# Thresholded attention and a gated MLP on one core: the threshold taken as the sign of differences scaled to 2^-126, one Exp per step over words read as int32, q and k transposed by half tiles, new lists of order

## The chip, the cores and the metric

The kernel runs on one core of one Trainium2 chip. The metric is the device time of one execution in microseconds; the time before is the median of three runs. The profile is one execution, with every instruction's start and duration on each engine: PE (TensorE, matmuls and transposes), PEld (its weight loads), DVE (VectorE), ACT (ScalarE), POOL (GpSimd) and SP, whose queue issues nearly all DMAs. Each engine works through its own row of instructions strictly in order, so an instruction that waits holds up everything behind it on its engine.

## The reference

Eight batches of eight heads, 576 positions, 64 dimensions a head. Scores more than tau = 0.02 below their row's maximum are dropped, the rest go through a softmax; its output goes into an MLP with spatial gating.

```python
scores = scale * np.matmul(q, k.transpose(0, 1, 3, 2))          # scale = 1/8
thresh = np.max(scores, axis=-1, keepdims=True) - tau
scores = np.where(scores >= thresh, scores, -1000000000.0)
scores = scores - np.max(scores, axis=-1, keepdims=True)
attn = np.exp(scores)
attn = attn / (np.sum(attn, axis=-1, keepdims=True) + 1e-09)
x = np.matmul(attn, v)                                          # then (8, 576, 512)
h = np.maximum(x @ w_in, 0.0)                                   # 512 -> 1024, split into u and v
v_n = (v - mu) / np.sqrt(var + 1e-06)
v_s = np.einsum('ts,bsd->btd', w_spatial, v_n) + b_spatial[None, :, None]
out = (u * v_s) @ w_out
```

## The kernel before

**Tiling.** The 64 heads are 32 pairs, four to a batch. A pair's 576 rows give four and a half blocks of 128; the half blocks of two neighbouring pairs share a step, so a batch has 18 steps and the whole kernel 144 (named g; the batch is the iteration). A step handles 128 rows of scores of both heads of a pair, 2 x 576 columns.

**A step.** The letters are those of the lists. S and Y (`part`, L830) make the scores on PE as float32 products of 64x64 tiles in one of two PSUM tiles `s`, three banks each. M (`top`, L859) is a DVE operation for each head that copies 576 scores from PSUM into the ring tile `e` and takes their maximum into `peak`, in SBUF; its second instruction reads the accumulator out. B (`shift`) makes the negative of the maximum plus tau (`negm`), on POOL (L873) or on DVE (L869). Then a step goes one of two ways, given by the table `WAYS`. In way "a" (102 of 144 steps) E and F are an ACT Prelu for each head (L890), which multiplies what is below the threshold by 1e30, and Z (L925) is one Exp over both heads into `p` in float16. In way "n" (42 steps) E and F are already the Exps (L887), and two DVE operations make the threshold: C (`keep`, L909) a mask, A (`pick`, L918) the bitwise AND into `p`. T sends `p` through a DMA transpose into `pT`. P (L505 to L524) multiplies `pT` with v and a column of ones; i (a reciprocal, L545) and p (a product, L548) divide by the sum on DVE.

**Beside the steps.** q and k of a pair are cast into the order of the blocks on POOL (sq, L306), transposed on PE (QA for q, QB for k, four 128x128 float32 transposes each, L448, into one of the two PSUM tiles `f`), and copied out into `qkT` by qa and qb, q times 1/8 (L428 on ACT, L422 on DVE), k as it is (L430, L424). QR, qr and kd do the same for the half blocks (L467, L460). The MLP of the batch before runs between: v with its mean and variance (L656 to L708), u, the gating product s and the output o. All of these share the two `f` tiles, each of one bank.

**Order.** Nothing schedules at run time. `ORDER` has a list of tokens for each batch and `LAST` four for the end; `run_token` issues the instructions of a token, each to its engine's row, so the lists set the order on every engine. A letter d ahead of an eviction puts it on DVE instead of ACT. The wait of an instruction on another engine is a semaphore that the framework places where a tile is written and read.

Of the kernel before, what the change touches and what calls it, by code (L numbers as in the profile page):

```python
# [34 lines left out]
(  # L35
# [18 lines left out]
(  # L54
# [117 lines left out]
(  # L172
# [1090 lines left out]
```

## Time and profile before

| | value |
|---|---|
| time, median of three runs | 429.21 us (428.72 to 431.87) |
| the profiled execution's own time | 429.39 us |
| its span in the trace | 427.6 us |
| POOL, DVE, ACT instructions | 469, 1035, 567 |
| DMA moved, mean rate | 88.18 MB, 206 GB/s |
| transposes of p by DMA | 141, 4.4 us from issue to landing |

The span runs from the first to the last instruction in the trace; 1.8 us of the execution lie outside it. A busy time is the union of an engine's instructions, so that the sums of groups, which overlap by some tens of nanoseconds at their ends, come to more. PE's instructions are pipelined and their ends modelled: a busy PE is not PE at its peak. Views used below are the page's sums by engine and its chain of waits, the groups of instructions by line, the answers for a single line with smallest, median and largest duration, the busy times by stretch of the span, and the timeline.

### The profile page before, as it was taken

What the parts mean: (1) busy time and instruction counts of PE and PEld (TensorE: products, weight loads), DVE (VectorE), ACT (ScalarE), POOL (GpSimd) and SP (SyncE); (2) the same over time, 40 slices, a digit from 0 to 9 for tenths busy, and PEclk for the clock granted to TensorE, in tenths of its full rate; (3) what the DMA queues carried; (4) which work ended last, traced back from release to release, by engine and by line L of the source; (5) the groups of instructions that cost most, each with busy time, mean ns of one, the idle gap of its engine ahead of it and who ended that gap; (6) DMA issues with size and microseconds to landing.
All of it is one profiled execution on the core that took longest, in us unless ns stands there. A gap on an engine that the chain in (4) does not pass through costs nothing.

```text
span 427.6 us, 13266 instructions
## 1 busy us (share of the span) xinstructions
PE 405.0 (95%) x4978; PEld 253.3 (59%) x5029; DVE 384.0 (90%) x1035; ACT 386.1 (90%) x567; POOL 191.4 (45%) x469
## 2 busy tenths in 40 slices
PE   8778978999999999999999999999999999999995
PEld 4456655566555675575665657656665666565642
DVE  6999989999899899989999999989999989999562
ACT  4999979999999999999999999999999999999362
POOL 2566437763246633554235631374233753255020
PEclk9999999999999999999999999999999999999999
DMA  7999999999999999998999989999989999989913
GB/s 196 288 280 182 263 273 227 168 182 195 239 265 171 214 213 188 204 210 227 214 165 280 211 165 252 217 221 210 236 138 229 228 214 206 160 150 214 180 57 117
DMA packets 224703, 88.18 MB, mean 206 GB/s; under 512 B 195648, under 2 KB 220352, under 8 KB 224640
## 3 DMA queue, kind: packets, MB, share of 16 engines
q1 hardware_dynamic: 224192, 86.75, 102.3%
q8 instruction: 39, 0.64, 0.6%
q10 hardware_dynamic: 368, 0.33, 0.2%
q0 software_dynamic: 80, 0.26, 0.2%
q14 instruction: 24, 0.20, 0.2%
HBM read 32.79 MB, written 9.44 MB: 99 GB/s over the span
## 4 chain that ended last, share of the span: by engine, by line
PE 62%; DVE 11%; ACT 9%; DMA 7%; issue 5%; POOL 3%; SPq 1%; POOLq 0%; DVEq 0%; ACTq 0%
PE s L830 25%; DVE e L859 7%; PE f L752 6%; DMA pT<-p 6%; PE f L448 5%; PE f L510 5%; PE f L723 4%; PE f L656 4%; ACT e L890 3%; PE f L781 3%; ACT e L887 2%; PE f L505 2%; ACT p L925 1%; DMA xT<-xn 1%; PE f L641 1%
## 5 line engine op out<-in xcount | busy, mean ns | idle before, releaser
L859 DVE CUSTOM_DVE_ANT_0 e<-s,zero 128x576 f32<-128x576 f32 x288 | 204.3, 752 | 5.8 <-PE s L830 1.4
L830 PE MATMUL s<-qkT 64*64 64x160 f32 (+1 forms) x2304 | 172.9, 413 | 4.5 <-DVE peak L859 3.7
L890 ACT ACTIVATE e<-e,negm 128x576 f32<-128x576 f32 x204 | 148.3, 766 | 4.8 <-PE s L830 2.3
L830 PEld LDWEIGHTS s<-qkT 64*64 64x64 f32 x2304 | 105.3, 132 | 53.2 <-issue 19.1
L925 ACT ACTIVATE p<-e 128x1152 f16<-128x1152 f32 x102 | 117.1, 1157 | 0.8
L873 POOL TENSOR_SCALAR negm<-peak 128x2 f32<-128x2 f32 x93 | 21.5, 231 | 133.3 <-DVE peak L859 89.7
L887 ACT ACTIVATE e<-e,negm 128x576 f16<-128x576 f32 x84 | 62.4, 767 | 2.0 <-POOL negm L873 1.3
L510 PE MATMUL f<-v,pT 128*128 128x65 bf16 x984 | 44.6, 194 | 0.0
L510 PEld LDWEIGHTS <-pT 128*128 128x128 f16 x1024 | 41.9, 98 | 2.4 <-issue 0.6
L918 DVE TENSOR_TENSOR p<-e 128x576 int32<-128x576 int32 x42 | 34.4, 822 | 0.5
L752 PE MATMUL f<-wsT,vn 128*128 128x512 bf16 x121 | 31.9, 380 | 0.9 <-DVE qkT L424 0.2
L505 PE MATMUL f<-v,pT 128*128 128x130 bf16 x123 | 27.2, 221 | 4.0 <-DMA pT<-p 3.9
L333 POOL CAST v<-vl 128x512 bf16<-128x512 f32 x32 | 21.3, 666 | 18.6 <-PE s L830 17.5
L708 POOL TENSOR_SCALAR vn<-vrel,rs,nm 128x512 bf16<-128x512 f32 (+1 forms) x35 | 27.9, 798 | 3.6
L723 PE MATMUL f<-xT,w_in 128*128 128x512 bf16 x102 | 28.5, 380 | 1.0 <-ACT qkT L430 0.3
L656 PE MATMUL f<-w_in,xT 128*128 128x512 bf16 x98 | 27.0, 380 | 1.4 <-DMA xT<-xn 0.3
L548 DVE TENSOR_TENSOR xn<-f,r 128x384 bf16<-128x384 f32 x46 | 25.2, 554 | 0.7
L781 PE MATMUL f<-w_o,gT 128*128 128x512 bf16 x94 | 25.1, 379 | 0.4
L859 DVE DVE_READ_ACCUMULATOR2_ANT peak<- 128x1 f32 x288 | 23.9, 83 | 0.0
L306 POOL COPY qn<-ql 128x512 f32<-128x512 f32 x31 | 19.7, 636 | 5.9 <-DMA ql<-in_q_dram 2.7
L752 PEld LDWEIGHTS <-vn 128*128 128x128 bf16 x140 | 12.8, 98 | 15.5 <-issue 3.1
L448 PE MATMUL f<-identf,kn 128*128 128x128 f32 x124 | 19.8, 282 | 2.2 <-DVE qkT L424 1.5
(175 smaller groups left out, 560.2 us busy)
## 6 DMA issues: line engine op xcount, KB each, us to landing
vl<-in_v_dram SPq DMA_DIRECT2D x16, 512.0 KB, 5.2
ql<-in_q_dram SPq DMA_DIRECT2D x15, 512.0 KB, 5.5
kl<-in_k_dram SPq DMA_DIRECT2D x15, 512.0 KB, 5.7
out_dram<-oo SPq DMA_DIRECT2D x12, 512.0 KB, 4.2
pT<-p SPq DMA_TRANSPOSE x141, 4.4
uT<-in_moe_w_in_dram SPq DMA_DIRECT2D x3, 512.0 KB, 6.4
uT<-in_moe_w_spatial_dram SPq DMA_DIRECT2D x2, 576.0 KB, 6.8
vx<-in_v_dram SPq DMA_DIRECT2D x16, 64.0 KB, 3.8
```

The source lines that it names most:

```text
L448: nc.tensor.transpose(out=t[:, c * P:(c + 1) * P], in_=nat[i][which][:, c, :], identity=identf)
L505: nc.tensor.matmul(out=t[:, at:at + 130], lhsT=pt[:, 4, rows], rhs=vt[:, 4:6, :].rearrange("p b d -> p (b d)"), start=True, stop=False)
L510: nc.tensor.matmul(out=t[:, at + 65 * h:at + 65 * h + 65], lhsT=pt[:, 5 * h + j, rows], rhs=vt[:, 6 * h + j, :], start=False, stop=(h == 1 ...
L656: nc.tensor.matmul(out=t, lhsT=x_of(b, f, slice(c * P, (c + 1) * P)), rhs=w_in[:, f, 512:1024], start=(f == 0), stop=(f == 3))
L723: nc.tensor.matmul(out=t, lhsT=w_in[:, m, f * P:(f + 1) * P], rhs=x_of(b, m, slice(0, 512)), start=(m == 0), stop=(m == 3))
L752: nc.tensor.matmul(out=t, lhsT=vn[:, c, f * P:(f + 1) * P], rhs=wsT[:, c, 0:512], start=(c == 0), stop=(c == 4))
L781: nc.tensor.matmul(out=t[:n], lhsT=gs[b][:, f, c * P:c * P + n], rhs=w_o[:, f, :], start=(f == 0), stop=(f == 3))
L830: made.append(nc.tensor.matmul(out=s_ring[g % 2][halves[k], at[h] + lo:at[h] + hi], lhsT=qks[n][halves[h], 0, m:m + 64], rhs=qks[n][halves ...
L859: nc.vector.tensor_tensor_reduce(out=e_ring[g % 3][:, h, :], in0=view(s_ring[g % 2], at[h], [[1, S]]), in1=zero.broadcast_to([P, S]), scal ...
L887: nc.scalar.activation(out=half_e(g)[0][:, h, :], in_=s, func=ACT.Exp, bias=bias_, scale=scale if steps[g][1] == 4 else 1.0)
L890: nc.scalar.activation(out=e, in_=s, func=ACT.Prelu, bias=bias_, scale=scale if steps[g][1] == 4 else 1.0, alpha=1e30)
L925: nc.scalar.activation(out=numerators(g), in_=e_ring[g % 3].rearrange("p h s -> p (h s)"), func=ACT.Exp)
```

## The change

The threshold moves off ACT. M now multiplies by 1/8 while it copies, and its accumulator goes to the first two columns of the step's own PSUM tile `s`. B is one DVE operation for each step: maximum minus tau, from PSUM into `thr`. E and F, one for each head, compute (score - thr) * 2^-126 in place in `e`, on POOL, or on DVE where the token has a d (180 and 108 of 288). A score above the threshold then is a tiny positive float whose bits, read as an integer, are the difference times 2^23; one below has its sign bit set and reads as a large negative integer. Z, for all 144 steps, is one ACT Exp over 1152 such words read as int32, times 2^-23, minus tau. `WAYS`, C and A are gone. The ring of `e` grows from three tiles to four, that of `p` shrinks from ten to nine.

q and k of a pair are transposed together (QX): each 128x128 block as two transposes of 64 rows, the upper rows into one `f` tile and the lower rows into the other, 16 for a pair where 8 were; qx and qy then copy one `f` tile each, half of q and half of k. q is no longer scaled there. At the start, two tiles go once through the same chain of operations, on POOL and on DVE, and the constant -0.5 (`mhalf`) comes out of that. All lists are new; evictions are nearly all on ACT now.

```diff
+    NE, NP = 4, 9
-    def qk_main(i, which):
+    def qk_main(i):
         def mm():
-            t = hold["t"] = bank()
-            for c in range(4):
-                nc.tensor.transpose(out=t[:, c * P:(c + 1) * P], in_=nat[i][which][:, c, :],
-                                    identity=identf)
+            hold.extend(bank() for _ in range(2))
+            for c in range(8):
+                w, n = divmod(c, 4)
+                for r in range(2):
+                    nc.tensor.transpose(
+                        out=hold[r][:, 64 * c:64 * c + 64], in_=nat[i][w][halves[r], n, :],
+                        identity=identf[halves[r], halves[r]])
+        def ev(r):
+            dst = qk_of(i)[:, :, 64:S].rearrange("p w (c s) -> p w c s", c=4)
+            evict(dst[:, :, :, 64 * r:64 * r + 64],
+                  hold[r].rearrange("p (w c s) -> p w c s", w=2, c=4))
...
+    def top(g):
+        peak[g] = s_ring[g % 2][:, 0:2]
+        for h in range(2):
             nc.vector.tensor_tensor_reduce(
-                in1=zero.broadcast_to([P, S]), scale=1.0, scalar=float("-inf"),
+                in1=zero.broadcast_to([P, S]), scale=scale, scalar=float("-inf"),
                 op0=ALU.add, op1=ALU.max, accum_out=peak[g][:, h:h + 1])
+    def bound(g):
+        thr[g] = small.tile([P, 2], F32, name="thr")
+        nc.vector.tensor_scalar(out=thr[g], in0=peak[g], scalar1=-float(tau), scalar2=None,
+                                op0=ALU.add)
     def spread(g, h):
+        e = e_ring[g % NE][:, h, :]
+        (nc.vector if on_vector[0] else nc.gpsimd).tensor_scalar(
+            out=e, in0=e, scalar1=thr[g][:, h:h + 1], scalar2=2.0 ** (SHIFT - 149),
+            op0=ALU.subtract, op1=ALU.mult)
     def exps(g):
-        nc.scalar.activation(out=numerators(g), in_=e_ring[g % 3].rearrange("p h s -> p (h s)"),
-                             func=ACT.Exp)
+        nc.scalar.activation(out=numerators(g),
+                             in_=e_ring[g % NE].rearrange("p h s -> p (h s)").bitcast(I32),
+                             func=ACT.Exp, bias=wrap, scale=2.0 ** -SHIFT)
...
+        for n, eng in enumerate((nc.gpsimd, nc.vector)):
+            t = e_ring[n][:, 0, :]
+            nc.vector.memset(t, 2.0 ** -100)
+            eng.tensor_scalar(out=t, in0=t, scalar1=zero, scalar2=2.0 ** -30,
+                              op0=ALU.subtract, op1=ALU.mult)
+            nc.scalar.activation(out=t, in_=t.bitcast(I32), func=ACT.Identity, scale=-2.0 ** -20)
+        nc.vector.tensor_tensor(out=mhalf, in0=e_ring[0][:, 0, 575:576],
+                                in1=e_ring[1][:, 0, 575:576], op=ALU.max)
```

SHIFT is 23 here. How the rows stand, at three places; names end in the number of the buffer, `s_96` and `s_97` are the two score tiles, `f_91` and `f_92` the two shared ones.

PE where a pair of the middle batches is transposed, before: eight full transposes behind scores of two steps.

```order
L830 MATMUL s_96<-qkT 64x416 x4
L830 MATMUL s_97<-qkT 64x160 x2
L830 MATMUL s_97<-qkT 64x416 x4
L448 MATMUL f_91<-identf,kn 128x128 x4
L448 MATMUL f_92<-identf,qn 128x128 x4
L830 MATMUL s_96<-qkT 64x160 x2
```

The same kind of place after; sixteen rows of the last kind follow one another, eight of q and eight of k, in turn into the two tiles.

```order
L810 MATMUL s_96<-qkT 64x160 x2
L810 MATMUL s_96<-qkT 64x416 x4
L810 MATMUL s_96<-qkT 64x160 x2
L440 MATMUL f_92<-identf,qn 128x64
L440 MATMUL f_91<-identf,qn 128x64
```

Each transpose has 64 rows in and 64 columns out of the identity, and both `f` tiles are taken at once.

DVE at its start, before, up to the copies of the first k and q:

```order
L1185 MEMSET zero 128x1
L1188 MEMSET ntau 128x1
L1189 MEMSET mhalf 128x1
L1191 CAST identb<-identf 128x128
L1192 CAST identh<-identf 128x128
L321 COPY kn<-kl_139 128x512
L321 COPY qn<-ql_138 128x512
```

And after; the maximum (L1128) waits for two ACT instructions, of which one waits for POOL.

```order
L1120 MEMSET zero 128x1
L1121 MEMSET wrap 128x1
L1124 MEMSET e_106 128x576
L1124 MEMSET e_107 128x576
L1125 TENSOR_SCALAR e_107<-e_107,zero 128x576
L1128 TENSOR_TENSOR mhalf<-e_106,e_107 128x1
L1131 CAST identb<-identf 128x128
L1132 CAST identh<-identf 128x128
L308 COPY kn<-kl_138 128x512
L308 COPY qn<-ql_137 128x512
```

Four operations of `e` and `mhalf` now stand ahead of the first copies of k and q.

DVE within a middle batch, before (M is named ISA here, two rows for each head):

```order
L859 ISA e_109,peak<-s_97,zero 128x576
L859 ISA peak 128x1
L909 TENSOR_SCALAR e_107<-e_107 128x2x576
L424 COPY oo<-f_91 128x512
L675 BN_STATS st<-vrel 128x6
L918 TENSOR_TENSOR p_111<-e_107 128x576
L859 ISA e_107,peak<-s_96,zero 128x576
```

And after:

```order
L846 TENSOR_SCALAR thr<-s_97 128x2
L665 BN_STATS st<-vrel 128x6
L538 TENSOR_TENSOR xn<-f_91,r 128x384
L665 BN_STATS st<-vrel 128x6
L669 BN_AGGR mv<-st 128x2
L852 TENSOR_SCALAR e_106<-e_106,thr 128x576
L838 ISA e_107,s_97<-s_97,zero 128x576
```

The mask, the AND and the copy of the output are gone from this row; the threshold and a spread of `e` stand in it. POOL beside it, before, where it normalises v (rs, nm, vn):

```order
L703 TENSOR_SCALAR nm<-mv,rs 128x1
L708 TENSOR_SCALAR vn_136<-vrel,rs,nm 128x512
L460 COPY qkT<-qkT 64x64
L873 TENSOR_SCALAR negm<-peak 128x2 x2
L696 TENSOR_SCALAR rs<-mv 64x1
L701 TENSOR_TENSOR rs<-rs,mhalf 64x1
```

And after:

```order
L693 TENSOR_SCALAR nm<-mv,rs 128x1
L698 TENSOR_SCALAR vn_136<-vrel,rs,nm 128x512
L852 TENSOR_SCALAR e_108<-e_108,thr 128x576
L452 COPY qkT<-qkT 64x64
L689 TENSOR_SCALAR rs<-ss 128x1
L691 TENSOR_TENSOR rs<-rs,mhalf 128x1
```

Where POOL had operations on two columns it now has operations on 576, between those of the MLP. In all, DVE has 144 of the small threshold operations; 56 of them wait for PE, because in their list the scores of the step two later, which go into the same `s` tile, stand ahead of them.

More of the change, by code (lines that the diff above doesn't have):

```diff
@@ L1 @@
-import math
 from contextlib import ExitStack
@@ L13 @@
 I32 = mybir.dt.int32
-U16 = mybir.dt.uint16
 AX = mybir.AxisListType
@@ L214 @@
     P = 128
+    NE, NP = 4, 9
+    tau = min(float(tau), 128.0)
+    SHIFT = 23
+    while 2 * tau >= 2.0 ** (24 - SHIFT):
+        SHIFT -= 1
     const = ctx.enter_context(tc.tile_pool(name="const", bufs=1))
@@ L241 @@
     identh = const.tile([P, P], F16, name="identh")
-    ntau = const.tile([P, 1], F32, name="ntau")
-    ctau = const.tile([P, 1], F32, name="ctau")
+    wrap = const.tile([P, 1], F32, name="wrap")
+    used = const.tile([P, 1], F32, name="used")
     mhalf = const.tile([P, 1], F32, name="mhalf")
     zero = const.tile([P, 1], F32, name="zero")
-    raised = const.tile([P, 2, 2], F32, name="raised")
     warm = const.tile([P, P], BF16, name="warm")
-    e_ring = [const.tile([P, 2, S], F32, name=f"e{i}") for i in range(3)]
-    p_ring = [const.tile([P, 1152], F16, name=f"p{i}") for i in range(10)]
+    e_ring = [const.tile([P, 2, S], F32, name=f"e{i}") for i in range(NE)]
+    p_ring = [const.tile([P, 1152], F16, name=f"p{i}") for i in range(NP)]
     pT_ring = [const.tile([P, 9, P], F16, name=f"pT{i}") for i in range(12)]
@@ L434 @@
     rest_late = (0, 1, 2)
+    halves = [slice(64 * k, 64 * k + 64) for k in range(2)]
     def qk_of(i):
@@ L440, in qk_of @@
         return qks[i]
[L442 to L443 removed]
+    def qk_main(i):
+        hold = []
         def mm():
[L446 to L456 removed]
+            hold.extend(bank() for _ in range(2))
[9 more added lines that the diff above has]
+                  hold[r].rearrange("p (w c s) -> p w c s", w=2, c=4))
+        return "act", mm, lambda: ev(0), lambda: ev(1)
     def rest_first(eng, t):
@@ L494, in first @@
         turn(tq, 0, 0, 0)
-        nc.scalar.mul(out=qkt[:, 0, 64:192], in_=tq[:, 0:P], mul=scale)
+        nc.scalar.copy(out=qkt[:, 0, 64:192], in_=tq[:, 0:P])
         for c in range(1, 4):
             turn(tm, P * (c - 1), 0, c)
-        nc.scalar.mul(out=qkt[:, 0, 192:576], in_=tm[:, 0:384], mul=scale)
-    halves = [slice(64 * k, 64 * k + 64) for k in range(2)]
+        nc.scalar.copy(out=qkt[:, 0, 192:576], in_=tm[:, 0:384])
     def weigh(t, at, pt, vt, rows=slice(0, P)):
@@ L850, in scores_end @@
         follow(part(g, 1, 0, S - cut)[0], turned[g])
-    negm, peak = {}, {}
-    def top(g, heads=slice(0, 2)):
-        if g not in peak:
-            peak[g] = small.tile([P, 2], F32, name="peak")
-        for h in range(heads.start, heads.stop):
+    peak, thr = {}, {}
+    def top(g):
+        peak[g] = s_ring[g % 2][:, 0:2]
+        for h in range(2):
             nc.vector.tensor_tensor_reduce(
-                out=e_ring[g % 3][:, h, :], in0=view(s_ring[g % 2], at[h], [[1, S]]),
-                in1=zero.broadcast_to([P, S]), scale=1.0, scalar=float("-inf"),
+                out=e_ring[g % NE][:, h, :], in0=view(s_ring[g % 2], at[h], [[1, S]]),
+                in1=zero.broadcast_to([P, S]), scale=scale, scalar=float("-inf"),
@@ L862, in top @@
                 op0=ALU.add, op1=ALU.max, accum_out=peak[g][:, h:h + 1])
-    def shift(g, engine):
-        nm = negm[g] = small.tile([P, 2], F32, name="negm")
-        down = -(scale if steps[g][1] == 4 else 1.0)
-        if engine is nc.vector:
-            engine.scalar_tensor_tensor(out=nm, in0=peak[g], scalar=down,
-                                        in1=raised[:, 0 if way(g) == "a" else 1, :],
-                                        op0=ALU.mult, op1=ALU.add)
-        else:
-            engine.tensor_scalar(out=nm, in0=peak[g], scalar1=down,
-                                 scalar2=float(tau) + (0.0 if way(g) == "a" else half_step),
-                                 op0=ALU.mult, op1=ALU.add)
@@ L877, in half_e @@
-    def half_e(g):
-        t = e_ring[g % 3].bitcast(F16)
-        return t[:, :, 0:S], t[:, :, S:2 * S]
-    def spread(g, h):
-        s = e_ring[g % 3][:, h, :]
-        e, bias_ = e_ring[g % 3][:, h, :], negm[g][:, h:h + 1]
-        if way(g) in "nrs":
-            nc.scalar.activation(out=half_e(g)[0][:, h, :], in_=s, func=ACT.Exp,
-                                 bias=bias_, scale=scale if steps[g][1] == 4 else 1.0)
-        elif on_act(g):
-            nc.scalar.activation(out=e, in_=s, func=ACT.Prelu, bias=bias_,
-                                 scale=scale if steps[g][1] == 4 else 1.0, alpha=1e30)
-        else:
-            nc.scalar.activation(out=e, in_=s, func=ACT.Exp, bias=bias_)
@@ L928, in turn_p @@
     def turn_p(g):
-        nc.sync.dma_start_transpose(out=pT_ring[g % 12], in_=p_ring[g % 10])
+        nc.sync.dma_start_transpose(out=pT_ring[g % 12], in_=p_ring[g % NP])
     staged = []
@@ L1116, in run_token @@
         relay = nc.gpsimd
-        if name[0] in "agv" and name[1] in "GB":
+        if name[0] in "agv" and name[1] == "G":
             relay = {"a": nc.scalar, "g": nc.gpsimd, "v": nc.vector}[name[0]]
@@ L1123, in run_token @@
         kind = name.rstrip("0123456789")
-        a = [int(x) for x in name[len(kind):]] if kind not in "SGYMHKBEFZWCAT" else []
-        g = 18 * b + int(name[len(kind):]) if kind in "SGYMHKBEFZWCAT" else 0
+        a = [int(x) for x in name[len(kind):]] if kind not in "SGYMBEFZT" else []
+        g = 18 * b + int(name[len(kind):]) if kind in "SGYMBEFZT" else 0
         if b >= B or g >= len(steps):
-            return
-        if kind in stepwise and way(g) not in stepwise[kind]:
             return
@@ L1131, in run_token @@
         m = 2 * b + a[0] if a else 0
-        if kind in "SGYMHKEFBZWCAT":
-            {"S": scores, "G": lambda g: turn_bank(g, relay), "Y": scores_end, "M": top, "E": lambda g: spread(g, 0),
-             "F": lambda g: spread(g, 1), "H": lambda g: top(g, slice(0, 1)),
-             "K": lambda g: top(g, slice(1, 2)), "B": lambda g: shift(g, relay), "Z": exps, "W": mask, "C": keep, "A": pick, "T": turn_p}[kind](g)
-        elif kind in ("QA", "QB", "qa", "qb"):
-            task("q", i, kind[1] in "Bb")[1 + (kind[0] == "q")]()
+        if kind in "SGYMBEFZT":
+            {"S": scores, "G": lambda g: turn_bank(g, relay), "Y": scores_end, "M": top, "B": bound,
+             "E": lambda g: spread(g, 0), "F": lambda g: spread(g, 1), "Z": exps,
+             "T": turn_p}[kind](g)
+        elif kind in ("QX", "qx", "qy"):
+            task("q", i)[1 + ("QX", "qx", "qy").index(kind)]()
         elif kind in ("QR", "qr", "kd"):
@@ L1185 @@
         nc.vector.memset(zero, 0.0)
-        nc.gpsimd.memset(raised[:, 0], float(tau))
-        nc.gpsimd.memset(raised[:, 1], float(tau) + half_step)
-        nc.vector.memset(ntau, -float(tau))
-        nc.vector.memset(mhalf, -0.5)
-        nc.scalar.activation(out=ctau, in_=ntau, func=ACT.Exp)
+        nc.vector.memset(wrap, -float(tau))
+        for n, eng in enumerate((nc.gpsimd, nc.vector)):
[6 more added lines that the diff above has]
+                                in1=e_ring[1][:, 0, 575:576], op=ALU.max)
+        nc.scalar.activation(out=used, in_=wrap, func=ACT.Exp)
         nc.vector.tensor_copy(out=identb, in_=identf)
```

48 lines of the change are left out of this document (4 added, 44 removed), and 276 rows, old and new, of tables (LAST, ORDER).

## The prediction

> **What bounds the kernel now.** I read the page's sums and its chain of waits first, then the stretches of the span, then the groups.
>
> ```profile
> span 427.6 us, 13266 instructions
> PE 405.0 (95%) x4978; PEld 253.3 (59%) x5029; DVE 384.0 (90%) x1035; ACT 386.1 (90%) x567; POOL 191.4 (45%) x469
> ...
> PE 62%; DVE 11%; ACT 9%; DMA 7%; issue 5%; POOL 3%; SPq 1%; POOLq 0%; DVEq 0%; ACTq 0%
> ```
>
> ```profile
> 0.00:10.00 10.00, 8.41 (x69) 4.81 (x69) 6.54 (x31) 3.72 (x7) 2.42 (x12) 1.00 0.72 193
> 10.00:60.00 50.00, 41.33 (x595) 28.11 (x593) 47.11 (x129) 48.59 (x69) 29.08 (x66) 1.00 1.17 247
> 160.00:210.00 50.00, 49.44 (x583) 30.36 (x588) 46.09 (x127) 47.76 (x68) 21.11 (x50) 1.00 1.11 206
> ...
> 392.00:410.00 18.00, 17.27 (x219) 10.52 (x218) 11.14 (x29) 9.62 (x17) 1.22 (x4) 1.00 0.87 188
> 410.00:427.60 17.60, 12.91 (x96) 6.41 (x96) 7.83 (x21) 7.69 (x15) 3.31 (x5) 1.00 0.22 75
> ```
>
> The columns are stretch, length, then PE, PEld, DVE, ACT and POOL busy, the granted clock, DMA share and rate. Three engines are nearly full at once: in a middle stretch PE has 49.4 of 50 us, ACT 47.8, DVE 46.1, and POOL alone has room. The chain is mostly PE's, with 20% on DVE and ACT. At 10 to 60 us ACT is the fullest and PE waits 8.7 us. The granted clock is 1.00 throughout. So an engine that is relieved gives time only as far as the other two allow.
>
> **The change, part by part.** Rows of what goes, and of what comes nearest to what is new:
>
> ```profile
> L859 DVE CUSTOM_DVE_ANT_0 e<-s,zero 128x576 f32<-128x576 f32 x288 | 204.3, 752 | 5.8 <-PE s L830 1.4 <-POOL rs L701 0.8 <-ACT qkT L498 0.7
> L890 ACT ACTIVATE e<-e,negm 128x576 f32<-128x576 f32 x204 | 148.3, 766 | 4.8 <-PE s L830 2.3 <-POOL negm L873 1.8
> L925 ACT ACTIVATE p<-e 128x1152 f16<-128x1152 f32 x102 | 117.1, 1157 | 0.8
> L887 ACT ACTIVATE e<-e,negm 128x576 f16<-128x576 f32 x84 | 62.4, 767 | 2.0 <-POOL negm L873 1.3 <-DVE negm L869 0.6
> L918 DVE TENSOR_TENSOR p<-e 128x576 int32<-128x576 int32 x42 | 34.4, 822 | 0.5
> L909 DVE TENSOR_SCALAR e<-e 128x1152 uint16<-128x1152 f16 x42 | 19.8, 474 | 1.3 <-ACT e L887 0.9
> L873 POOL TENSOR_SCALAR negm<-peak 128x2 f32<-128x2 f32 x93 | 21.5, 231 | 133.3 <-DVE peak L859 89.7 <-PE s L830 7.5 <-ACT e L890 6.8
> L869 DVE SCALAR_TENSOR_TENSOR negm<-peak,raised 128x2 f32<-128x2 f32 x51 | 10.3, 202 | 1.3 <-PE s L830 0.6
> L422 DVE TENSOR_SCALAR qkT<-f 128x512 f32<-128x512 f32 x13 | 8.9, 685 | 0.5 <-PE f L448 0.5
> L430 ACT COPY oo<-f 128x512 f32<-128x512 f32 x13 | 7.5, 580 | 1.2 <-PE f L781 1.1
> ```
>
> *ACT.* Out go 148.3 + 62.4 + 117.1 = 327.8 us; in come 144 Exps of the form of L925 (144 x 1.157 = 166.6; I take int32 words at the price of float32 ones) and some 72 evictions that DVE had, two thirds of them of 128x512, at about 0.58 us or less: near 38 us. 386 - 328 + 167 + 38 = 263 us. ACT has room from then on. By itself that gives no time, since PE and DVE stand beside it; the exception is 10 to 60 us, where ACT leads with 48.59 and DVE follows with 47.11. The gain there lies between 1.5 us (down to DVE's load) and 8.7 us (PE's whole idle time); I take 4, nearer to the low end, since DVE keeps its load.
>
> *DVE, what goes.* 42 x 0.822 + 42 x 0.474 + 51 x 0.202 = 64.7 us, and those 72 evictions (24 halves of qkT at 0.685, the rest between 0.27 and 0.685): near 40 us. Together 105.
>
> *DVE, what comes.* 144 thresholds of two columns at the median of the small operations below, 0.16 to 0.19: 25 us. 108 spreads of 576 float32 columns:
>
> ```profile
> L545 DVE RECIPROCAL r<-f x46: 155/193/197, 36.0 to 400.3; 128x6 f32<-128x6 f32 x46
> L321 DVE COPY kn<-kl x1: 427/427/427, 3.4 to 3.4; 128x512 f32<-128x512 f32 x1
> L970 DVE TENSOR_SCALAR vn<-vrel,rstd,shift x2: 547/742/936, 412.4 to 413.1; 128x512 bf16<-128x512 f32 x2
> L918 DVE TENSOR_TENSOR p<-e x42: 725/758/1476, 12.1 to 395.7; 128x576 int32<-128x576 int32 x42
> L708 POOL TENSOR_SCALAR vn<-vrel,rs,nm x35: 761/767/1202, 77.3 to 389.4; 128x512 bf16<-128x512 f32 x28, 64x512 bf16<-64x512 f32 x7
> L873 POOL TENSOR_SCALAR negm<-peak x93: 190/192/719, 9.0 to 393.0; 128x2 f32<-128x2 f32 x93
> ```
>
> A copy of 512 costs 0.427, the same with two per-partition scalars 0.547 undisturbed. With one scalar and 576 columns that is between 0.43 and 0.62 (0.547 x 576/512); I take 0.52, so 108 x 0.52 = 56 us. But L970's second instance took 0.936, L918 up to 1.476, L708 up to 1.202: such DVE operations and POOL's long ones shut each other out of SBUF and wait whole instructions. L918's mean lies 64 ns above its median (822 - 758), while POOL ran long operations (the groups below, 89 us) for 21% of the span.
>
> ```profile
> L333 POOL CAST v<-vl 128x512 bf16<-128x512 f32 x32 | 21.3, 666 | 18.6 <-PE s L830 17.5
> L708 POOL TENSOR_SCALAR vn<-vrel,rs,nm 128x512 bf16<-128x512 f32 (+1 forms) x35 | 27.9, 798 | 3.6
> L306 POOL COPY kn<-kl 128x512 f32<-128x512 f32 x31 | 20.1, 647 | 0.9 <-DMA kl<-in_k_dram 0.7
> L306 POOL COPY qn<-ql 128x512 f32<-128x512 f32 x31 | 19.7, 636 | 5.9 <-DMA ql<-in_q_dram 2.7 <-PE s L830 1.9
> ```
>
> *POOL.* 180 spreads. From 0.192 for two columns to 0.767 for 512 the slope is 1.13 ns a column, so 576 cost 0.84: 151 us. POOL goes to 191 - 21 + 151 = 321 us, and its long operations from 89 to 240 us, 58% of some 415. The 64 ns then grow 2.8 times: 0.18 us for each of 108 spreads on DVE, 19 us, and about as much for POOL, which ends near 340. Bounds of that wait: nothing, or a whole POOL spread each time (108 x 0.84 = 91 us). The Trainium skill (GPSIMD Engine Reference, Elementwise — side-by-side cycle accounting) puts a light body at 1.03 cycles an element at 1.2 GHz; by that, an estimate, a spread would be 0.19 + 0.49 = 0.68 us and POOL's total 29 us lower. The nearest row here, L708, has two operations on each element as the spread has, and costs 1.13 ns; the measured slope stays.
>
> DVE in all: 384 - 105 + 25 + 56 + 19 = 379. It is where it was, within the error of these terms, and stays at nine tenths. DMA moves the same bytes; at 247 GB/s in one stretch it has shown more than the 88.18 MB in 415 us, 212 GB/s, ask for.
>
> *PE.* Two transposing groups a pair go, for 31 pairs, sixteen half transposes come:
>
> ```profile
> 100.60 2.17 PE L830 MATMUL s<-qkT 64*64 64x160 f32 x32
> 102.70 0.66 PE L448 MATMUL f<-identf,qn 128*128 128x128 f32 x4
> 103.19 0.22 PE L505 MATMUL f<-v,pT 128*128 128x130 bf16 x1
> ...
> L448 PE MATMUL f<-identf,kn 128*128 128x128 f32 x124 | 19.8, 282 | 2.2 <-DVE qkT L424 1.5 <-POOL negm L873 0.7
> L448 PEld LDWEIGHTS f<-identf,kn 128*128 128x128 f32 x124 | 13.4, 141 | 9.1 <-issue 2.5 <-DVE qkT L424 1.7 <-DVE st L675 1.1
> L830 PE MATMUL s<-qkT 64*64 64x160 f32 (+1 forms) x2304 | 172.9, 413 | 4.5 <-DVE peak L859 3.7 <-ACT qkT L430 0.6
> L830 PEld LDWEIGHTS s<-qkT 64*64 64x64 f32 x2304 | 105.3, 132 | 53.2 <-issue 19.1 <-DVE peak L859 9.7 <-POOLq L845 1.7
> ```
>
> Four full transposes hold PE from 102.70 to 103.19, 0.49 us, so 62 groups cost 30 us. The scores show that tiles in different rows and columns of the array run side by side: 2304 matmuls of 0.413 us in 172.9 us, and their loads too, 0.132 each in 105.3. If upper and lower half run beside each other and stream 64 columns instead of 128, the 30 us halve: bounds 0 and -15; I take -13, for a few changes of shape. PE's chain share makes this a term in full: -13.
>
> *The start.* The copy of the first k (L321) began at 3.4. Now two memsets of 576 (one of 512 took 0.485), a POOL spread (0.84), a shut-out DVE spread and two ACT operations of 0.766 stand ahead of it: 2.6 + 0.55 + 0.84 + 1.5 + 0.5 brings it to about 6.0. The q copy, at 4.2 before, comes at about 6.5, and no work covers this: +2.3, between +1 and +3.
>
> *Sum.* 427.6 - 13 - 4 + 2.3 = 412.9 of span; 1.8 lie outside it (429.39 - 427.6), so 414.7. The profiled execution stands 0.2 above the median, so about 415.
>
> **The rivals.**
>
> *Slower: POOL and DVE shut each other out.* Without the waits DVE has 384 - 105 + 25 + 56 = 360 us. What DVE cannot use is 3.5 us at the start and 16.6 after 392 us, 20 in all, so at 413 us of DVE the run is over 1% slower. That is a mean wait of (413 - 360)/108 = 0.49 us for each spread. L970's one instance and L918's largest waited 0.4 and 0.7, but their mean was 0.06. At 0.6 us: 360 + 65 + 20 + 1.8 = 447.
>
> *Slower: weight loads one after another.* 124 loads took 13.4 us, 0.108 each. If sixteen loads of a pair can't overlap, a pair takes 16 x 0.108 = 1.73 us in place of 0.98: +23, and 427.6 + 23 - 4 + 2.3 + 1.8 = 451. The Trainium skill (TensorE: Matmul & The Clock Gate, LDWEIGHTS (loading the stationary operand)) has the rule that a load's time goes by its columns, not its rows, so that halving the rows saves nothing; no row here has a load of 64 rows and 128 columns. Against this rival stand the loads of the scores, 46 ns apart (105.3/2304).
>
> *About the same: the saving on PE is lost.* Either the halves don't run side by side (427.6 - 4 + 2.3 + 1.8 = 428), or the 56 thresholds that wait for PE hold DVE, with the maxima behind them and scores behind those: at 0.25 us each 14 us, and 429. For it: DVE and PE are both full. Against: in most places a further M of 1.7 us stands between.
>
> *Faster than forecast.* With ACT's evictions prompt, PE's hidden gaps shrink until DVE alone bounds: 379 + 20 + 1.8 = 401. For it: 20% of the chain lies on ACT and DVE.
>
> **How the numbers follow.** Forecast 0.50 (own range 408 to 423); faster still, 0.18; about the same 0.18; shut-out 0.10; loads 0.04. About 1% is what a measurement can tell from no change, so faster holds 0.50 + 0.18 = 0.68, same 0.18, slower 0.10 + 0.04 = 0.14. The range leaves out the slower cases and the end of the fastest: 402 to 428.
>
> **What would show it.** In the changed profile ACT should be near 263 us, DVE near 380, POOL near 340, each half transpose group of a pair 0.5 to 0.6 us on PE, a DVE spread some 0.7 in the mean with a minimum near 0.52, a POOL spread 0.84, the first k copy at 6 us. The forecast is wrong if DVE's spreads exceed 1 us in the mean, if POOL passes 90% of the middle stretches, or if idle time of DVE ahead of the threshold's line, put down to PE, passes 10 us.

## The result, and the profile after

| | before | changed |
|---|---|---|
| time, median of 4 runs | 428.97 us (428.46 to 431.87) | 655.46 us (653.31 to 655.69) |
| span of the profiled execution | 427.6 us | 651.3 us |
| granted TensorE clock, mean | 1.00 | 0.861 |

The changed kernel takes 1.525 times as long (95% interval 1.517 to 1.532). The forecast was 415 us, and no rival came near: the slowest stood at 451. Executions of two kernels below, the one without the trial and the one with the halves alone, fall into a faster and a slower group; their times and ratios are those of the faster one.

The page of the changed kernel, its sums by engine (busy us, share of the span, instructions), five rows of slices, and the chain of waits:

```profile
PE 484.1 (74%) x5222; PEld 277.8 (43%) x5277; DVE 403.3 (62%) x1083; ACT 293.6 (45%) x395; POOL 567.6 (87%) x555
...
PE   6776776588757795786856866787787885787967
...
DVE  5665675477755685585733764567775975475744
ACT  2344455465254443454434544255524761345533
POOL 2999998998999989999999999999998999989911
PEclk9687887778889798897968897888987988787989
...
POOL 61%; PE 18%; issue 11%; DVE 6%; ACT 3%; DMA 0%; POOLq 0%; DVEq 0%; ACTq 0%
POOL e L852 47%; PE s L810 7%; DVE e L838 3%; POOL vn L698 2%; ACT p L862 2%; POOL rs L691 2%; POOL v L320 2%; POOL kn L293 1%; PE f L771 1%; POOL qn L293 1%; PE f L713 1%; POOL v L326 1%; PE f L742 1%; PE f L500 1%; POOL qkT L452 1%
```

POOL, at 45% before, is the only engine that is full: its row of slices holds eights and nines nearly from end to end, while ACT's stand at 1 to 7 and those of PE and DVE mostly at 5 to 8. Line 852, the spread, alone makes 47% of the chain. The groups of instructions by line of the same kernel, and the answer for line 852 on POOL and then on DVE (smallest, median, largest duration):

```profile
L852 POOL TENSOR_SCALAR e<-e,thr 128x576 f32<-128x576 f32 x180 | 402.6, 2236 | 26.8 <-DVE thr L846 10.3
L862 ACT ACTIVATE p<-e,wrap 128x1152 f16<-128x1152 int32 x144 | 179.4, 1254 | 262.7 <-POOL e L852 251.7
L852 DVE TENSOR_SCALAR e<-e,thr 128x576 f32<-128x576 f32 x108 | 70.2, 669 | 4.7 <-PE s L810 4.4
L838 DVE DVE_READ_ACCUMULATOR2_ANT s<- 128x1 f32 x288 | 40.6, 141 | 0.0
```

```profile
L852 POOL TENSOR_SCALAR e<-e,thr x180: 2207/2212/2543, 16.9 to 618.4; 128x576 f32<-128x576 f32 x180
...
L852 DVE TENSOR_SCALAR e<-e,thr x108: 478/528/1020, 20.2 to 608.4; 128x576 f32<-128x576 f32 x108
```

The same instruction costs 0.528 us on DVE and 2.212 on POOL, where the forecast had 0.84. Smallest and median lie 5 ns apart, so it isn't a wait that comes and goes: each one takes that long. 180 x (2.236 - 0.84) = 251 us more than reckoned. Counted apart from that, ACT's Exp waits 251.7 us for POOL. The list of waits (us in total, times, longest; ACTq is ACT's sequencer) shows how it goes round:

```profile
ACT p L862 <- POOL e L852: 251.7, 88, 10.3
DVE e L838 <- ACT p L862: 86.8, 32, 7.4
PEld s L810 <- ACTq L825: 49.5, 22, 7.5
DVE e L838 <- PE s L810: 43.7, 29, 4.9
```

The Exp waits for the spread, the maximum waits for the Exp to free one of four e tiles, and TensorE's next scores wait behind both; TensorE is idle in pieces of up to 7.5 us, and its mean clock is 0.861, where the profile before had 1.00.

### The profile page after: what moved, and what is told of

It is laid out like the page before. It is cut to its first block, busy times and chain, and to the rows that moved or that the text cites. A ratio compares the mean times of both kernels' runs of the same rounds, so it can differ in the third digit from the quotient of the medians.

```text
span 651.3 us, 13760 instructions
## 1 busy us (share of the span) xinstructions
PE 484.1 (74%) x5222; PEld 277.8 (43%) x5277; DVE 403.3 (62%) x1083; ACT 293.6 (45%) x395; POOL 567.6 (87%) x555
## 4 chain that ended last, share of the span: by engine, by line
POOL 61%; PE 18%; issue 11%; DVE 6%; ACT 3%; DMA 0%; POOLq 0%; DVEq 0%; ACTq 0%
POOL e L852 47%; PE s L810 7%; DVE e L838 3%; POOL vn L698 2%; ACT p L862 2%; POOL rs L691 2%; POOL v L320 2%; POOL kn L293 1%; PE f L771 1%; POOL qn L293 1%; PE f L713 1%; POOL v L326 1%; PE f L742 1%; PE f L500 1%; POOL qkT L452 1%
## 5 line engine op out<-in xcount | busy, mean ns | idle before, releaser
L852 POOL TENSOR_SCALAR e<-e,thr 128x576 f32<-128x576 f32 x180 | 402.6, 2236 | 26.8 <-DVE thr L846 10.3
L862 ACT ACTIVATE p<-e,wrap 128x1152 f16<-128x1152 int32 x144 | 179.4, 1254 | 262.7 <-POOL e L852 251.7
L810 PE MATMUL s<-qkT 64*64 64x160 f32 (+1 forms) x2304 | 223.2, 470 | 83.6 <-ACTq L825 36.1
L852 DVE TENSOR_SCALAR e<-e,thr 128x576 f32<-128x576 f32 x108 | 70.2, 669 | 4.7 <-PE s L810 4.4
L417 ACT COPY qkT<-f 128x512 f32<-128x512 f32 (+1 forms) x85 | 38.6, 484 | 21.6 <-PE f L440 15.9
L838 DVE DVE_READ_ACCUMULATOR2_ANT s<- 128x1 f32 x288 | 40.6, 141 | 0.0
L846 DVE TENSOR_SCALAR thr<-s 128x2 f32<-128x2 f32 x144 | 21.7, 158 | 29.7 <-PE s L810 27.8
L440 PE MATMUL f<-identf,qn 64*128 64x64 f32 x248 | 18.8, 261 | 24.1 <-ACT vrel L655 6.9
L658 ACT ACTIVATE vrel<-f 128x512 f32<-128x512 f32 (+1 forms) x28 | 16.4, 592 | 17.5 <-PE f L646 12.0
L413 ACT ACTIVATE uT<-f 128x512 bf16<-128x512 f32 (+1 forms) x33 | 18.0, 551 | 12.8 <-PE f L713 9.2
```

Source lines behind the costliest of these rows:

```text
L417: nc.scalar.copy(out=out, in_=in_)
L440: nc.tensor.transpose(out=hold[r][:, 64 * c:64 * c + 64], in_=nat[i][w][halves[r], n, :], identity=identf[halves[r], halves[r]])
L810: made.append(nc.tensor.matmul(out=s_ring[g % 2][halves[k], at[h] + lo:at[h] + hi], lhsT=qks[n][halves[h], 0, m:m + 64], rhs=qks[n][halves ...
L838: nc.vector.tensor_tensor_reduce(out=e_ring[g % NE][:, h, :], in0=view(s_ring[g % 2], at[h], [[1, S]]), in1=zero.broadcast_to([P, S]), sca ...
L852: (nc.vector if on_vector[0] else nc.gpsimd).tensor_scalar(out=e, in0=e, scalar1=thr[g][:, h:h + 1], scalar2=2.0 ** (SHIFT - 149), op0=ALU ...
L862: nc.scalar.activation(out=numerators(g), in_=e_ring[g % NE].rearrange("p h s -> p (h s)").bitcast(I32), func=ACT.Exp, bias=wrap, scale=2. ...
```

## The experiments

Why is the spread slow on POOL? Theory 1: the results are subnormal, that is, below 2^-126, the smallest normal float32. Rival 2: the form of the operation (which two operations, in which order). Rival 3: VectorE, at work beside POOL, holds it up. Line numbers of experiments are those of the changed kernel unless the text says otherwise.

**Results of ordinary size.**

```
-            ... scalar2=2.0 ** (SHIFT - 149), op0=ALU.subtract, op1=ALU.mult)
+            ... scalar2=2.0 ** -40, op0=ALU.subtract, op1=ALU.mult)
-                             func=ACT.Exp, bias=wrap, scale=2.0 ** -SHIFT)
+                             func=ACT.Exp, bias=wrap, scale=2.0 ** -27)
```

> The changed kernel with the spread's multiplier 2^-40 in place of 2^-126 and the Exp's scale 2^-27 in place of 2^-23: the same instructions at the same places, but no result of a spread lies below the smallest normal number. The threshold and the softmax are then not the reference's (all values are off). Theory 1 (POOL is slow because its results are subnormal): a POOL spread takes 0.77 to 0.90 us instead of 2.21, POOL's busy time falls from 568 to about 330 us, the granted clock comes back to 1.00 and the time is 420 to 445 us. Rival 2 (the form subtract by a scalar per row, then multiply by a constant, with an f32 result, is slow on POOL whatever the numbers): 2.2 us a spread and 650 to 656 us. Rival 3 (VectorE shuts POOL out): the least duration would fall below 1 us while the mean stays near 2.2, time 600 to 655 us.

Measured: 635.55 us, 1.481 times before (1.474 to 1.487). Its group of spreads on POOL:

```profile
L852 POOL TENSOR_SCALAR e<-e,thr 128x576 f32<-128x576 f32 x180 | 401.1, 2240 | 13.7 <-DVE thr L846 7.4
```

2.240 us with normal results: theory 1 falls. The time is 20 us below the changed kernel's, and below the 650 expected of rival 2. The spreads' own price did not change; POOL stands idle for 68.7 us of the span here and for 83.7 in the changed kernel, and why was not followed up.

**All spreads on VectorE.**

```
-        (nc.vector if on_vector[0] else nc.gpsimd).tensor_scalar(
+        nc.vector.tensor_scalar(
```

(made by a d ahead of every E and F of the lists)

> The changed kernel with all 288 spreads on VectorE (108 before), at the same places of the lists; the numbers are the changed kernel's, still below the smallest normal number. Theory 1 and rival 2 (the price is GpSimd's alone): a spread on VectorE stays at 0.48 to 0.53 us, VectorE's busy time goes from 403 to 403 + 180 x 0.50 - 20 (less waiting for POOL) = about 470 us, POOL's from 568 to about 165, and the time is 480 to 510 us, with VectorE as the bound. If VectorE paid for such numbers as well, a spread there would stand well over 0.6 us and the time over 530.

Measured: 536.85 us, 1.251 times before (1.245 to 1.257), above the 480 to 510 expected. From its sums by engine and its groups:

```profile
PE 443.9 (83%) x5277; PEld 259.4 (49%) x5277; DVE 470.1 (88%) x1263; ACT 291.8 (55%) x395; POOL 182.1 (34%) x375
...
L852 DVE TENSOR_SCALAR e<-e,thr 128x576 f32<-128x576 f32 x288 | 150.2, 563 | 1.7 <-PE s L810 1.1
```

119 us come back with the spreads off POOL, and a spread stays at 0.563 us in the mean, below the 0.6 that would have shown a price on VectorE: the price is GpSimd's alone. VectorE's 470 us are as expected, and it is now the fullest engine; why the time lies above the expectation, and above the 530 named as a sign of a price on VectorE, was not followed up.

**The forms, one by one.** Behind the end of the kernel before, pairs of operations with their own lines (each writes e or p; `one` and `zero` are columns):

```
1240 gpsimd  (src - one) * 2^-126          1258 gpsimd  as 1240, 72 of 576 not zero
1243 gpsimd  (src - one) * 1.0             1261 gpsimd  copy of subnormal words
1246 gpsimd  (src - one) * 2^-110          1263 gpsimd  src - one
1249 gpsimd  src * 2^-126 + zero           1266 vector  (few - one) * 2^-126
1252 gpsimd  src * one + zero              1269 vector  (few - one) * 1.0
1255 gpsimd  as 1252, f16 out
1273 scalar  Exp of int32 words, bias a column; 1276 of f32, bias a column; 1278 of f32
```

> The kernel before, and behind its end pairs of single operations on 128 x 576 words, each with its own line; nothing of the computation is changed, and the time is some 20 to 40 us above that of before. GpSimd, f32 to f32, in this order: subtract and multiply with a result of 2^-126 x 0.01 (subnormal), with a normal result x 1, x 2^-110; multiply by a constant then add a column, subnormal; multiply and add by columns, f32 and f16 out; subtract and multiply with 72 of 576 results subnormal and the rest zero; a copy of subnormal words; subtract alone. Theory 1: about 2.2 us where all results are subnormal, 0.7 to 0.9 where they are normal, and between or low at 72 of 576. Rival 2: about 2.2 us for subtract and multiply with any numbers, under 1 for multiply and add. VectorE's subtract and multiply: 0.5 us with both kinds of result. ScalarE's Exp over 1152: from int32 words 1.25 us, from f32 with a bias 1.16, f32 alone 1.16; if the int32 reading costs nothing in itself, all three agree.

The run took 468.39 us. Its groups by line:

```profile
L1243 POOL TENSOR_SCALAR e<-e,one 128x576 f32<-128x576 f32 x2 | 4.4, 2211 | 0.2
...
L1240 POOL TENSOR_SCALAR e<-e,one 128x576 f32<-128x576 f32 x2 | 4.4, 2208 | 2.0 <-DVE e L1235 1.9
...
L1273 ACT ACTIVATE p<-e,ntau 128x1152 f16<-128x1152 int32 x2 | 2.5, 1254 | 33.1 <-DVE e L1271 33.1
L1276 ACT ACTIVATE p<-e,ntau 128x1152 f16<-128x1152 f32 x2 | 2.5, 1254 | 0.1
L1278 ACT ACTIVATE p<-e 128x1152 f16<-128x1152 f32 x2 | 2.3, 1162 | 0.1
L1252 POOL TENSOR_SCALAR e<-e,one,zero 128x576 f32<-128x576 f32 x2 | 1.6, 822 | 0.2
...
L1249 POOL TENSOR_SCALAR e<-e,zero 128x576 f32<-128x576 f32 x2 | 1.5, 746 | 0.2
...
L1266 DVE TENSOR_SCALAR e<-e,one 128x576 f32<-128x576 f32 x2 | 1.0, 520 | 27.5 <-POOL e L1263 27.4
```

Subtract and multiply takes 2.21 us whether the result is subnormal or not; multiply and add takes 0.75 even where it is. Rival 2 holds, and rival 3 falls: from line 1243 on no other engine is at work beside POOL. On ScalarE the int32 words cost nothing (lines 1273 and 1276 agree); the column of the bias costs 92 ns (lines 1276 and 1278).

**Which part of the form.** Again behind the kernel before:

```
1240 (src - one) * 0.5     1248 (src - 0.5) * 0.25     1254 src - low, two tiles
1242 (src + one) * 0.5     1250 src + one              1256 src * low, two tiles
1244 src * 0.5 - one       1252 src + low, two tiles   1258 as 1240, 64 columns
1246 src * 0.5 + one                                   1260 as 1246, 64 columns
```

> The kernel before, and behind its end pairs of single GpSimd operations, each with its own line, all with results of ordinary size; nothing of the computation is changed. If it is the subtraction that GpSimd is slow at: subtract then multiply 2.2 us with a column or a constant, multiply then subtract also above 1.7, add then multiply 0.75 to 0.85, and the subtraction of two tiles slower than their sum. If it is the order (an addition ahead of a multiplication): add then multiply is as slow as subtract then multiply, and multiply then subtract as quick as multiply then add. At 64 columns in place of 576, a per-column price of 2.2/576 = 3.8 ns gives 0.3 to 0.4 us, a fixed price about 1.6.

The run took 463.04 us. Its groups by line:

```profile
L1244 POOL TENSOR_SCALAR e<-e,one 128x576 f32<-128x576 f32 x2 | 4.4, 2215 | 0.2
...
L1250 POOL TENSOR_SCALAR e<-e,one 128x576 f32<-128x576 f32 x2 | 3.5, 1728 | 0.2
L1254 POOL TENSOR_TENSOR e<-e 128x576 f32<-128x576 f32 x2 | 2.8, 1396 | 0.2
...
L1252 POOL TENSOR_TENSOR e<-e 128x576 f32<-128x576 f32 x2 | 2.8, 1395 | 0.2
L1246 POOL TENSOR_SCALAR e<-e,one 128x576 f32<-128x576 f32 x2 | 1.5, 746 | 0.2
L1242 POOL TENSOR_SCALAR e<-e,one 128x576 f32<-128x576 f32 x2 | 1.5, 745 | 0.2
...
L1258 POOL TENSOR_SCALAR e<-e,one 128x64 f32<-128x64 f32 x2 | 1.0, 509 | 0.2
L1260 POOL TENSOR_SCALAR e<-e,one 128x64 f32<-128x64 f32 x2 | 0.6, 320 | 0.2
```

A subtraction in either place makes the two-operation form slow; multiply with add is quick in either order. Of two tiles, difference and sum cost the same, so it is not the arithmetic. Nor is it only the subtraction: an addition alone, one operation, takes 1.73, more than twice what addition with a multiplication takes. By the column it is (2210 - 509)/512 = 3.32 ns for subtract and multiply and (746 - 320)/512 = 0.83 ns for multiply and add. The Trainium skill (GPSIMD Engine Reference, Elementwise — side-by-side cycle accounting) has 1.03 cycles an element for a light body. At its 1.2 GHz, an estimate, the quick form's 0.83 ns are 1.00 cycle and agree, the slow form's 3.32 are 4.0 and do not: here the rule holds for some pairs of operations only.

**The spread with multiply and add.**

```
-    ... scalar1=-float(tau), scalar2=None, op0=ALU.add)
+    ... scalar1=-float(tau), scalar2=-2.0 ** (SHIFT - 149), op0=ALU.add, op1=ALU.mult)
-    out=e, in0=e, scalar1=thr[g][:, h:h + 1], scalar2=2.0 ** (SHIFT - 149), op0=ALU.subtract, op1=ALU.mult)
+    out=e, in0=e, scalar1=2.0 ** (SHIFT - 149), scalar2=thr[g][:, h:h + 1], op0=ALU.mult, op1=ALU.add)
```

> The changed kernel with the spread written as a multiplication by the constant 2^-126 and then the addition of a column that holds -threshold x 2^-126 (the threshold's operation makes that column, one instruction as before), on the same engines at the same places; the numbers stay below the smallest normal number. Theory 2 (GpSimd's price hangs on the form): a POOL spread takes 0.75 to 0.85 us instead of 2.21, POOL's busy time is 568 - 180 x 1.43 = about 310 us, the granted clock is near 1.00 again, and the time is that of my sum with the two prices it missed (reading the maximum into PSUM, +17 us on VectorE; the Exp with a bias, +14 us on ScalarE): 420 to 450 us. If the order of the two operations does not matter and GpSimd is slow for another reason that the separate measurement did not hold (the e tiles' place, VectorE beside it), it stays at 2.2 us and 650. VectorE's spread: 0.48 to 0.53 us undisturbed in either form, a mean of 0.60 to 0.75 with its waits for POOL.

Measured: 444.74 us, 1.035 times before (1.031 to 1.038). Its sums by engine, its clock and some of its groups:

```profile
PE 410.3 (92%) x5277; PEld 246.1 (55%) x5277; DVE 389.1 (88%) x1083; ACT 291.4 (66%) x395; POOL 309.7 (70%) x555
...
PEclk8899999999999999999999999999999999999998
...
L852 POOL TENSOR_SCALAR e<-e,thr 128x576 f32<-128x576 f32 x180 | 138.4, 769 | 66.1 <-DVE thr L846 44.6 <-PE s L810 2.1 <-DVE s L838 2.0
...
L852 DVE TENSOR_SCALAR e<-e,thr 128x576 f32<-128x576 f32 x108 | 63.8, 611 | 0.3
L838 DVE DVE_READ_ACCUMULATOR2_ANT s<- 128x1 f32 x288 | 40.4, 140 | 0.0
```

211 of the 226 us that the change cost are gone by the form of one operation. The other 15 are looked for in the next runs; TensorE is again the fullest engine.

**The maximum in SBUF, then also the Exp without its bias.** On the run with multiply and add:

```
-        peak[g] = s_ring[g % 2][:, 0:2]
+        peak[g] = small.tile([P, 2], F32, name="peak")
```

> The run with multiply-and-add spreads (444.7 us) with the maximum kept in SBUF, and the Exp with its bias column as the change has it. The run with both edits came to 437.3. If the maximum in PSUM made the difference (the accumulator's read 141 ns instead of 80, 288 times, and TensorE waiting for the threshold before it may write the bank again, 22 us in the waits), this run is at 436 to 439; if the Exp's bias did (97 ns, 144 times, on ScalarE, which is busy 66% of the span), it stays at 443 to 445.

and with it, in the second run:

```
-                             func=ACT.Exp, bias=wrap, scale=2.0 ** -SHIFT)
+                             func=ACT.Exp, scale=2.0 ** -SHIFT)
```

> The run with multiply-and-add spreads, and in it the maximum kept in SBUF instead of PSUM (as in the kernel before) and the Exp without its bias column (every numerator then is larger by the factor e^0.02, which the division by their sum takes out again). Expected: the accumulator's read 83 ns instead of 141 (-17 us of VectorE's time), the Exp 1157 ns instead of 1254 (-14 us of ScalarE's). If VectorE bounds the run with multiply-and-add, the time falls by 10 to 17 us; if TensorE or the ring of e tiles does, by 0 to 6.

Measured: 436.73 us with the first edit, 1.017 times before (1.011 to 1.023), and 437.31 with both, 1.017 (1.014 to 1.021). So the maximum's place is worth 8 us and the bias nothing that these runs can tell, though without it the Exp falls from 1254 to 1163 ns. The Trainium skill (ScalarE: Activation LUTs, What ACT_TABLE_LOAD costs) gives about 93 ns for each operand that is a column; the 91 here agree. In the run with the first edit alone:

```profile
L846 DVE TENSOR_SCALAR thr<-peak 128x2 f32<-128x2 f32 x144 | 32.4, 236 | 2.1 <-PE s L810 0.6
L838 DVE DVE_READ_ACCUMULATOR2_ANT peak<- 128x1 f32 x288 | 23.3, 81 | 0.0
...
PEld s L810 <- DVE peak L838: 10.7, 21, 1.3
PE s L810 <- DVE peak L838: 4.6, 9, 1.1
```

The read falls from 140 to 81 ns, the threshold behind it rises from 160 to 236 (144 times, so 11 of 17 us are given back on VectorE), and the scores now wait 10.7 + 4.6 = 15 us for VectorE's maxima and 2.4 for thresholds, instead of 13.7 + 15.6 + 6.9 + 3.5 = 40 for both. So VectorE's own work shrinks by 6 us, and the PSUM bank comes free one instruction earlier; which of the two makes how much of the 8 us, no run separates.

**Whole transposes.** On the run with multiply and add:

```
-                for r in range(2):
-                    nc.tensor.transpose(out=hold[r][:, 64 * c:64 * c + 64], in_=nat[i][w][halves[r], n, :], identity=identf[halves[r], halves[r]])
+                nc.tensor.transpose(out=hold[w][:, P * n:P * n + P], in_=nat[i][w][:, n, :], identity=identf)
...
+            evict(qk_of(i)[:, r, 64:S], hold[r])
```

> The run with multiply-and-add spreads, and in it q and k transposed by whole 128x128 tiles (8 in a group, one bank for q and one for k) instead of 16 by halves; all places, banks and sizes of the evictions stay. By the prediction a half-tile group takes half as long (62 half groups at 0.49 us = 30 us of busy time less), of which 13 us were to show in the total: so this run is 8 to 15 us slower than the one with multiply-and-add. If the halves don't run beside each other, or TensorE is not what the steps wait for, the two agree within 3 us.

Measured: 448.16 us, 1.044 times before (1.040 to 1.047), so the halves are worth 3.4 us. A pair's transposes in the timelines of the run with halves and of the one with whole tiles (start us, us):

```profile
121.94 0.46 PE L440 MATMUL f<-identf,qn 64*128 64x64 f32 x8
122.25 0.41 PE L440 MATMUL f<-identf,kn 64*128 64x64 f32 x8
122.59 0.76 PE L810 MATMUL s<-qkT 64*64 64x160 f32 x8
```

```profile
122.95 0.66 PE L439 MATMUL f<-identf,qn 128*128 128x128 f32 x4
123.44 0.60 PE L439 MATMUL f<-identf,kn 128*128 128x128 f32 x4
123.97 0.76 PE L806 MATMUL s<-qkT 64*64 64x160 f32 x8
```

To the next scores it is 0.65 us against 1.02. The groups over all 31 pairs, again first with halves, then whole:

```profile
L440 PE MATMUL f<-identf,qn 64*128 64x64 f32 x248 | 15.9, 236 | 0.5 <-DVE gT L759 0.3
...
L440 PE MATMUL f<-identf,kn 64*128 64x64 f32 x248 | 13.3, 223 | 0.0
```

```profile
L439 PE MATMUL f<-identf,qn 128*128 128x128 f32 x124 | 20.4, 287 | 0.4 <-DVE gT L755 0.3
L439 PE MATMUL f<-identf,kn 128*128 128x128 f32 x124 | 18.6, 273 | 0.0
```

That is 29.2 us against 39.0, some 10 us of TensorE's work. Twice as many transposes, each of half the columns, take three quarters of the time, so they do run side by side in part; 3.4 of the 10 us reach the end.

**Without the trial of small numbers at the start.** On the run with both edits, the fills, trial spreads, ScalarE operations and maximum that make -0.5 become one fill:

```
+        nc.vector.memset(mhalf, -0.5)
```

> The run with the maximum in SBUF and no bias, and ahead of the first copies no trial of small numbers any more: the two fills, the two trial spreads, the two ScalarE operations and the maximum that made -0.5 from them are one fill with -0.5. The first maximum began at 13.3 us against 7.5 before the change. If the trial operations make this gap, the first maximum comes at 7.5 to 9 us and the time falls by 4 to 6 us, to 431 to 434; if something else of the order does (the first step is now step 1, not step 0), it stays at 12 us or more and the time falls by less than 2.

Measured: 434.8 us (433.15 to 439.63), 1.014 times before (1.009 to 1.019), not told apart from 1.017. The first maximum does begin at 8.3 us instead of 13.3, so the trial makes that gap. The kept trace is of an execution of 440.43 us, longer than those: in it the 37th of the 288 maxima begins at 45.0 us against 50.1, the 73rd at 99.1 against 99.6. What becomes of the start's 5 us in the shorter executions it can't show, and that stays open.

**VectorE's spreads on ScalarE; thresholds on GpSimd.** Two attempts at a faster version, on the run without the trial. The second moves the thresholds of those 57 steps whose spreads are both on GpSimd:

```
+            nc.scalar.activation(out=e, in_=e, func=ACT.Identity, scale=2.0 ** (SHIFT - 149), bias=thr[g][:, h:h + 1])
```

> The run without the trial, and the 108 spreads that VectorE did done by ScalarE (Identity with the constant as its scale and the column as its bias), at the same places of the lists. VectorE loses 108 x 0.61 = 66 us of its 379, ScalarE gains 108 x 0.77 = 83 and comes to about 362; GpSimd, at 310, no longer meets VectorE's two-port operations. If VectorE is what TensorE waits for, the time comes to 420 to 430, under that of before; if TensorE's own 405 us are the bound with the lists as they stand, it stays within 3 us of the run without the trial; if ScalarE, which now waits for thresholds in its order, holds up the evictions, it is slower than that run by 5 us or more. (If ScalarE drops numbers this small, the softmax is not the reference's in these half steps; the time is not changed by that.)

```
-        nc.vector.tensor_scalar(
+        (nc.vector if g in spread_on_vector else nc.gpsimd).tensor_scalar(
```

> The run without the trial, and the threshold of those 57 of 144 steps whose halves are both spread by GpSimd made on GpSimd. VectorE loses 57 x 0.25 = 14 us, GpSimd gains 57 x 0.2 = 11. If VectorE's time counts, 4 to 10 us faster than the run without the trial; if TensorE is the bound, within 2 us.

Measured: 469.98 us, 1.094 times before (1.090 to 1.099), and 453.84 us, 1.058 (1.053 to 1.064). Both free VectorE (busy 320.9 and 372.3 us against 377.7) and both are slower: in the first, maxima wait 46.8 us for scores and 22.4 for the Exp, with 15.4 and 3.5 in the trace of the run that it was made from; in the second the Exp waits 53.4 us for POOL's spreads (20.6), and POOL's thresholds 32.4 for maxima. Here an instruction moved to another engine without a new order waits in that engine's row, and what stands behind it waits too.

**The halves alone.** The kernel before with half transposes, the lists changed by a rule and not planned anew:

```
-    "... S7:0 QA2:0 s3:2 L0:-1 Co3:2 Z4:0 Z5:0 dqa2:0 es3:2 G7:0 Y7:0 QB2:0 XP2:1 M7:0 dxp2:1 qb2:0 ..."
+    "... S7:0 s3:2 L0:-1 Co3:2 Z4:0 Z5:0 es3:2 G7:0 Y7:0 QX2:0 dqx2:0 qy2:0 XP2:1 M7:0 dxp2:1 ..."
```

> The kernel before with one part of the change alone: q and k transposed by half tiles into two banks, with the two evictions behind them, and the scale taken into the maximum's operation instead of q's eviction. In the lists QX stands where the two banks are free, near the later of the two places of QA and QB; the softmax is that of before. In the changed kernel with multiply-and-add spreads the halves took 10 us of TensorE's busy time (39.0 to 29.2) and 3.4 us of the time. If the same holds here, the time is 424 to 427, under both kernels; if TensorE gets the whole 10 us back, 418 to 421; if taking two banks at once makes TensorE wait for evictions (some 31 groups at 0.2 to 0.5 us, 6 to 15 us), it is 428 to 440, no gain.

Measured: 486.96 us (484.72 to 489.67), 1.133 times before (1.128 to 1.137), beyond all three. In the kept trace, of a longer execution of 498.70 us, TensorE's clock has a mean of 0.939, and evictions wait 23.5 + 15.3 us for half transposes. The run is 57 us slower than before, and halves and new places changed together in it, so it says nothing on the halves themselves; the run with whole transposes, with every place kept, is the one that counts.

No version beat the kernel before.

## Why the prediction was wrong

- **The step that failed:** "The nearest row here, L708, has two operations on each element as the spread has, and costs 1.13 ns; the measured slope stays." L708 is multiply and add; the spread was subtract and multiply, which no row of before showed on POOL at this width. 0.84 us became 2.24, 251 us of POOL's time, and the chain and the time followed. For this term the text also gave no upper bound: its only other value, 0.68, lay below. L708's own form, multiply and add with two columns, measured 0.822 alone at this width, and the spread with one column 0.769 in the kernel, so 0.84 was near for the form that it came from.
- **POOL at 340, full below 90%:** the sign named for a wrong forecast, POOL above 90% of the middle stretches, appeared (91.67 to 94.29 of each 100 us between 60 and 360). With the form changed POOL stands at 309.7 us.
- **DVE's spreads** were right undisturbed, at a median of 528 ns against 0.52 us. That the mean, 669, comes near the forecast 0.70 is partly luck, since POOL was busy far longer than reckoned; with the short POOL form it is 611, so the wait was 0.09 us and not 0.18. The rival of mutual exclusion, at 0.49 us of waiting, was not reached. DVE's total, 403 against 379, was missed mainly by the accumulator's read into PSUM (141 ns instead of 83, 17 us), which the change's line `peak[g] = s_ring[...]` showed and the sum passed over; the place of the maximum cost 8 us of time. The read in the kernel before:

```profile
L859 DVE DVE_READ_ACCUMULATOR2_ANT peak<- 128x1 f32 x288 | 23.9, 83 | 0.0
```

- **ACT at 263:** 293.6. The Exp took 1254 ns instead of 1157, 14 us, not for the int32 words but for the bias column, which L925 does not have. It did not count in the time: the run without it is no faster. The rest of the 31 us was not followed up.
- **PE, -13:** the halves do overlap, a pair taking 0.65 us against 0.5 to 0.6. The term was mis-sized: 10 us of work and 3.4 us of time, not 13 of both.
- **10 to 60 us, -4:** with multiply and add, from the first maximum to the 37th it was 39.8 us (12.9 to 52.7) against 39.4 before (7.5 to 46.9): nothing. With the maximum in SBUF it was 37.4 (13.3 to 50.8) and without the bias as well 36.8, so a gain of 2 to 2.6 was there behind the PSUM reads, in one execution of each.
- **The start, +2.3:** the first k copy came at 7.21 us, not 6.0, since the trial spread on POOL took 2.22 us as well; the first maximum came 5.8 us later, 3.8 by that copy and 2.1 behind it. There the first four transposes took 1.09 us in place of 0.60. A low clock after the idle start is the likely reason: it reads 0.55 from 8 to 12 us in the run with multiply and add, but 1.00 in the changed kernel's own trace, so this is not shown.
- **Weight loads one after another:** no. In the run with multiply and add, loads of 64 rows took 138 to 140 ns, as many as loads of 128 rows (141) before; but they overlap, 248 in 11 us. The Trainium skill (TensorE: Matmul & The Clock Gate, LDWEIGHTS (loading the stationary operand)) has the rule that rows don't count in a load's time, and the 138 to 141 ns agree.

With POOL's form right, the sum of 414.7 lacks 30 us to 444.7. The runs account for 8 (PSUM), 9.6 (halves), 3.1 (start: first maximum at 12.9 there, 5.4 late) and about 4 (10 to 60 us), if these simply add up; some 5 stay open.

## What to carry to other kernels

A duration may be carried from one instruction to another on GpSimd only if the operations are the same, not only their number, width and type; where no row shows the pair, the bound upward must be wide enough to flip the sign, and one short run of the single instruction settles it. A subtraction of a column, beside a multiplication, can be written as the addition of its negative; making the negative cost nothing here (the threshold took 160 ns instead of 158). When a slow instruction has smallest and median durations alike, look at the instruction first, then at what it waits for.
